# Expert mixture kernel: block 2's load, the last weights' raw buffers, the sums' steps, and the overflow path's form

## The chip, the cores and the metric

One core of a Trainium2 chip runs the whole program. The metric is the device time of one execution in microseconds (us). TensorE is called PE here (PEld is its weight load), VectorE DVE, ScalarE ACT, GpSimd POOL; SP is the engine whose queue issues most DMAs, in the order of the program.

## The reference

Attention with a causal mask and a position bias for 2304 tokens, then a mixture of 8 experts of which every token goes to two, then a gated layer:

```
x = attention(q, k, v, s)                     # 2304 tokens x 512
top2 = two largest of x @ w_gate + noise      # of 8 experts
for e in range(8):
    h = maximum(x[mask] @ w1[e], 0)           # 512 -> 1024
    out[mask] += weight * (h @ w2[e])         # 1024 -> 512
return (sigmoid(out @ w_gate2) * (out @ w_val2)) @ w_out2   # 512 -> 1536 -> 512
```

## The kernel before, in words

The program has three stages: attention and gating (to some 300 us of the span), the experts, and the gated layer, which the code calls `moe2`. Every float32 product is made of three matmuls on a high and a low part (`hh` and `hl`, `xh` and `xl`, `w[:, 0]` and `w[:, 1]`): ACT copies the high part, DVE or POOL subtracts to get the low one.

**The expert stage** is a loop over jobs; a job is one expert and one block `f` of 128 hidden columns. In each pass n of the loop PE does `mm1(n)` (lines 230 to 232, x times the first weights, into `h`), then `mm2s(n - 1)` (lines 244 to 246, into `y`). Between them ACT makes `hh` (line 233) and DVE `hl` (line 234) of the `h` just computed; `mm2s` of the next pass needs both. The order of the work on every engine is that of the code: nothing is reordered, and an instruction that waits holds up all that stands behind it on its engine or queue.

**The last expert** is split. Its first 8 passes take 384 tokens (three tiles), the last 8 the other 256 (two tiles). This text counts passes from the first of the second half: steps -8 to -1 and 0 to 7, so step k is pass `n == tail + k`. The second half takes the 8 weight blocks in another order: its steps 0 to 3 use weights that are still held, its steps 4 to 7 load theirs again. These four are the late weights.

**A weight block** is made by `weights` (lines 151 to 159): SP loads it raw into a buffer `wraw` (line 154), ACT makes its high part (line 157), POOL its low part (line 158). `start(n)` issues the load, `load(n)` starts it if need be and converts. `wraw` has two buffers in the pool `stage`, so a load waits until POOL has done with the block before the last. The last late block (step 7) has a buffer of its own, `tw`.

**Blocks of the gated layer.** `two` (class `Second`) prepares the first three weight blocks of `moe2` while the last expert runs. `block(f)` loads one raw into `ro` (line 526, 768 KB, two buffers), then converts it in three pieces: each is an ACT copy (line 517) and a DVE subtraction (line 521). The table `BLOCKS` says in which step which piece is made. Block 2 takes the `ro` buffer that block 0 leaves.

**The first tokens of the gated layer.** `after(j)` runs at the end of each step j from 0. `both(t)` loads the two halves `y` of the output of token tile t (line 348), DVE adds them (line 339), and `feed` transposes the sum on PE (line 576) and splits it into `xh` (ACT, line 584) and `xl` (DVE, line 586). `FEED = (4, 5, 7)` says in which step each tile's feed is made up; its transposes come one step later.

**The overflow path.** An expert has 640 slots; `overflow` does the tokens beyond them. Every engine loads a count (line 445) and branches (line 446). Here the count is zero, so the body is jumped over on every engine. The body holds 44 PE matmuls for one expert, with a loop around them, and is written out for each of the 8 experts.

Of the kernel before, what the change touches and what calls it, by code (L numbers as in the profile page):

```python
# [8 lines left out]
F32 = mybir.dt.float32  # L9
# [42 lines left out]
LOW_DVE = (3, 5, 6, 7, 16, 17)  # L52


BLOCKS = {-7: (0, 0), -6: (0, 1), -5: (1, 1), -3: (2, 2), -2: (2,)}
FEED = (4, 5, 7)
COMBO = 7 * 256

# [9 lines left out]
@with_exitstack  # L68
def attn_moe_moe2_kernel(ctx: ExitStack, tc: tile.TileContext, q, k, v, s, wgn, noise, wcat, w2cat, out):
    nc = tc.nc  # L70
    ctx.enter_context(tc.manual_schedule())
    const = ctx.enter_context(tc.tile_pool(name="const", bufs=1))


    xs = tc.dram_tile([E * CAP, XW], F32, name="xs")

    ys = tc.dram_tile([2 * N, DM], F32, name="ys")
    aux = tc.dram_tile([2, 2, NP, S], F32, name="aux")

    nc.scalar.preload_act_table_set("natural_log_exp_and_others")  # L80


    identf = const.tile([128, 128], F32, name="identf")
    identr = const.tile([128, 128], F32R, name="identr")
    identb = const.tile([128, 128], BF, name="identb")
    jp = const.tile([128, 128], I32, name="jp")
    nc.gpsimd.iota(jp, pattern=[[1, 128]], base=0, channel_multiplier=-1)
    nc.vector.tensor_scalar(identf, jp, 0.0, None, op0=OP.is_equal)
    nc.vector.tensor_copy(identb, identf)
    mask = const.tile([128, 192], BF, name="mask")  # L90
    nc.vector.tensor_scalar(mask[:, 0:128], jp, 0.0, NEG, op0=OP.is_gt, op1=OP.mult)
    for r in (slice(0, 64), slice(64, 128)):
        nc.vector.tensor_scalar(mask[r, 128:192], jp[r, r], 0.0, NEG, op0=OP.is_gt, op1=OP.mult)
    ltri = const.tile([128, 128], BF, name="ltri")
    ones = const.tile([128, 128], BF, name="ones")
    iota_d = const.tile([128, 8], F32, name="iota_d")
    carry = const.tile([128, 8], F32, name="carry")
    valid = const.tile([128, 5], F32, name="valid")
    wgt = const.tile([128, 4, 32], F32, name="wgt")
    nz = const.tile([128, 20, 8], F32, name="nz")  # L100
    tok = const.tile([128, 20], F32, name="tok")

    def iotas():
        nc.gpsimd.iota(iota_d, pattern=[[-1, 8]], base=8, channel_multiplier=0, allow_small_or_imprecise_dtypes=True)
        nc.gpsimd.iota(carry, pattern=[[CAP, 8]], base=0, channel_multiplier=0, allow_small_or_imprecise_dtypes=True)
        for b in range(B):

            for i, n, base in ((0, 4, b * 512), (4, 1, B * 512 + b * 64)):
                nc.gpsimd.iota(tok[:, 5 * b + i:5 * b + i + n], pattern=[[128, n]], base=base, channel_multiplier=1,
                               allow_small_or_imprecise_dtypes=True)  # L110

    def others():
        nc.vector.tensor_copy(identr, identf)
        nc.vector.tensor_scalar(ltri, jp, 0.0, None, op0=OP.is_gt)
        nc.vector.memset(ones, 1.0)
        nc.vector.memset(valid, 1.0)
        nc.vector.memset(valid[64:128, 4:5], 0.0)

    stage = ctx.enter_context(tc.tile_pool(name="stage", bufs=2))
    state = dict(identf=identf, identb=identb, mask=mask, ltri=ltri, ones=ones, iota_d=iota_d, carry=carry,  # L120
                 valid=valid, wgt=wgt, nz=nz, tok=tok, iotas=iotas, others=others)
    over = const.tile([128, E + 1], I32, name="over")
    cnt = const.tile([128, E], F32, name="cnt")

    def count():

        nc.gpsimd.iota(cnt, pattern=[[CAP, E]], base=SLOTS, channel_multiplier=0, allow_small_or_imprecise_dtypes=True)
        nc.vector.tensor_tensor(cnt, carry, cnt, op=OP.subtract)
        nc.vector.tensor_scalar(cnt, cnt, 0.0, 127.0, op0=OP.max, op1=OP.add)
        nc.vector.tensor_copy(over[:, 0:E], cnt)  # L130
        nc.vector.tensor_scalar(over[:, 0:E], over[:, 0:E], 7, None, op0=OP.logical_shift_right)
        nc.vector.tensor_copy(cnt, over[:, 0:E])
        nc.vector.tensor_reduce(cnt[:, 0:1], cnt, axis=AX.X, op=OP.max)
        nc.vector.tensor_copy(over[:, E:], cnt[:, 0:1])

    w2f = tc.dram_tile([FB2, 128, FF2], F32, name="w2f")
    gs = tc.dram_tile([FB2, 128, N - CT * 128], F32, name="gs")
    gates, res = ExitStack(), ExitStack()
    moe_pools = ExitStack()
    ring = moe_pools.enter_context(tc.tile_pool(name="ring", bufs=4, reuse_waits="tile"))  # L140
    w1 = {}
    blocks = [weights(nc, stage, ring, wcat, 0, f) for f in range(AHEAD)]
    ahead = [lambda f=f: w1.update({f: next(blocks[f])}) for f in range(AHEAD) for _ in range(2)]
    late = attention(tc, gates, ahead, q, k, v, s, wgn, noise, aux, xs, **state)
    with res:
        two, first = moe(tc, moe_pools, res, gates, stage, ring, w1, late, count, xs, ys, wcat, w2cat, w2f, identf, identr)
        overflow(tc, xs, ys, wcat, carry, over, identf)
        moe2(tc, two, first, ys, w2f, gs, identr, out)


def weights(nc, stage, pool, wcat, e, f, name="w", lo=None):

    r = stage.tile([128, 1024], F32, name="wraw")
    nc.sync.dma_start(r, wcat[e, f])
    yield
    w = pool.tile([128, 2, 1024], F32R, name=name)
    nc.scalar.activation(w[:, 0], r, AF.Copy)  # L157
    (lo or nc.gpsimd).tensor_tensor(w[:, 1], r, f32(w[:, 0]), op=OP.subtract)  # L158
    yield w


def moe(tc, pools, res, gates, stage, ring, W, late, count, xs, ys, wcat, w2cat, w2f, identf, identr):
# [4 lines left out]
    with pools as ctx:  # L167
# [17 lines left out]
        def start(n):  # L185
            e, f = jobs[n][0:2]
            lo = nc.vector if n in LOW_DVE else nc.gpsimd
            pool, name = (w0, f"w{f}") if n < FB and f >= 4 else (ring, "w")
            LD[n] = weights(nc, tw[0] if n == n_all - 1 else stage, pool, wcat, e, f, name, lo)
            next(LD[n])  # L190

        def load(n):
# [19 lines left out]
            nc.vector.tensor_tensor(lo, p, f32(hi), op=OP.subtract)  # L212

        def own_tokens(e, t0, t1):
            wt, row = owners(nc, xp, e, XR[e][:, t0:t1, DM:XW], t1 - t0)
            for t in range(t0, t1):
                OWN[e, t] = wt[:, t - t0:t - t0 + 1], row[:, t - t0:t - t0 + 1]

# [110 lines left out]
        def after(j):  # L329

            if j == 0:
                first.extend(two.x0.tile([128, 4, CT * 128], F32R, name=m, bufs=1) for m in ("xh", "xl"))
                y.update((i, both(i)) for i in range(2))
            if j == FEED[0] + 1:
                y[2] = both(2)
            for i, at in enumerate(FEED):
                if j == at:
                    p = ps.tile([128, 512], F32, name=f"y{i}")
                    nc.vector.tensor_tensor(y[i][0], y[i][0], y[i][1], op=OP.add)
                    turns[i] = feed(nc, y[i][0], p, identf, *(x[:, :, i * 128:(i + 1) * 128] for x in first))  # L340
                if at < j < at + 3:
                    next(turns[i])
# [34 lines left out]
        for n in range(FB, n_all):  # L377
# [16 lines left out]
                load(n + 3)  # L394
            if n == tail - 2:
                tw.append(ctx.enter_context(tc.tile_pool(name="tw", bufs=1, side="right", reuse_waits="tile")))
                for i in (4, 5, 7):
                    start(tail + i)
            if n == tail + 2:
                start(tail + 6)  # L400
            for f2 in BLOCKS.get(n - tail, ()):
                two.go(f2)
            if n == tail - 6:
                two.start(two.block, 2, 2)
            if n >= tail:
                after(n - tail)
# [17 lines left out]
    return two, first  # L424


def owners(nc, pool, e, x, n):

    g = pool.tile([128, 4, n], F32, name="own")
    row = pool.tile([128, n], I32, name="row")  # L430
    first, second, w, rf = (g[:, i] for i in range(4))
    nc.vector.tensor_scalar(first, x[:, :, 1], float(E - e), None, op0=OP.is_equal)
    nc.vector.tensor_scalar(second, x[:, :, 1], float(E - e), None, op0=OP.not_equal)
    nc.vector.scalar_tensor_tensor(rf, second, float(N), x[:, :, 0], op0=OP.mult, op1=OP.add)
    nc.vector.tensor_tensor(first, first, x[:, :, 2], op=OP.mult)
    nc.vector.tensor_tensor(second, second, x[:, :, 3], op=OP.mult)
# [2 lines left out]
    return w, row  # L439


def overflow(tc, xs, ys, wcat, carry, over, identf):

    nc = tc.nc
    some = nc.values_load(over[0:1, E:E + 1], min_val=0, max_val=(N - SLOTS) // 128)
    with tc.If(some > 0):
        with ExitStack() as ctx:
# [12 lines left out]
            for e in range(E):  # L460
                nc.gpsimd.indirect_dma_start(
                    out=xs, out_offset=bass.IndirectOffsetOnAxis(ap=endi[:, e:e + 1], axis=0), in_=zt, in_offset=None)
            for e in range(E):
                n = nc.values_load(over[0:1, e:e + 1], min_val=0, max_val=(N - SLOTS) // 128)
                with tc.For_i(0, n, 1) as i:
                    x = sb.tile([128, 1, XW], F32, name="x")
                    nc.sync.dma_start(x[:, 0], xs[bass.ds(i * 128 + (e * CAP + SLOTS), 128), :])
                    w, row = owners(nc, sb, e, x[:, :, DM:XW], 1)
                    p = ps.tile([128, 512], F32, name="t")
                    for c in range(4):  # L470
                        nc.tensor.transpose(p[:, c * 128:(c + 1) * 128], x[:, 0, c * 128:(c + 1) * 128], identf)
# [2 lines left out]
                    y = ps.tile([128, DM], F32, name="y", bufs=1)  # L474
                    for f in range(FB):
                        wt = sb.tile([128, 1024], F32, name="w")
                        nc.sync.dma_start(wt, wcat[e, f])
                        h = ps.tile([128, 512], F32, name="h")
                        for c in range(4):
                            k = slice(c * 128, (c + 1) * 128)  # L480
# [880 lines left out]
```

## Time and profile before

| | us |
|---|---|
| median of 3 runs | 1159.85 (1159.49 to 1161.51) |
| the profiled execution | 1169.18 |
| its span (first to last instruction) | 1167.3 |
| PE busy in the span | 1109.1 (95%) |
| DVE, ACT, POOL busy | 717.4, 527.8, 367.2 |
| last expert, steps -8 to 7, on PE | 653.77 to 727.35 |
| first matmul of `moe2` | 733.16 |

The times below are microseconds from the start of the profiled span. A matmul takes its issue interval on the path, not the length shown: the lengths of neighbours overlap.

### The profile page before, as it was taken

Reading aid. Unit: us, or ns where it says so; the run is one execution under the profiler, and the core shown is the slowest. Engines: PE = TensorE matmul, PEld = TensorE weight load, DVE = VectorE, ACT = ScalarE, POOL = GpSimd, SP = SyncE. Lnnn points to the kernel's source line nnn. Section 1 sums busy time; section 2 is a strip of 40 time slices with the busy share of each in tenths; the row PEclk is TensorE's granted clock in tenths of the full one; section 3 lists DMA queues with packets and bytes.
Section 4 is the critical chain, followed back from the end, with each engine's and each line's share of the span. In section 5 each row is a group of like instructions: output and inputs, shape, how many; then the busy total and the mean of one; then the engine's idle time right before and its main releaser. Section 6 shows DMA issues by size and latency. Waiting matters only on the chain. (4 is left out here: it accounts for less than half of the span.)

```text
span 1167.3 us, 16831 instructions
## 1 busy us (share of the span) xinstructions
PE 1109.1 (95%) x6193; PEld 940.3 (81%) x6193; DVE 717.4 (61%) x1227; ACT 527.8 (45%) x1073; POOL 367.2 (31%) x375
## 2 busy tenths in 40 slices
PE   6999899699999999999999978899999999999998
PEld 4676566478899999999999867899888898988886
DVE  5777788573467687887683444376788567752221
ACT  5887677522333333333333423365566456532211
POOL 2110442405235353535353525012443333300000
PEclk8999999889999999999999989899999999999999
DMA  6798665326555756565754433572554345354442
GB/s 223 247 321 274 197 211 161 107 85 208 192 154 176 252 187 231 176 239 181 252 162 136 168 117 126 147 198 81 163 163 127 109 158 176 116 159 114 133 120 64
DMA packets 84849, 198.77 MB, mean 170 GB/s; under 512 B 7986, under 2 KB 31538, under 8 KB 84756
## 3 DMA queue, kind: packets, MB, share of 16 engines
q1 hardware_dynamic: 76308, 174.54, 46.2%
q0 software_dynamic: 8304, 22.89, 6.5%
q8 instruction: 51, 0.84, 0.3%
q14 instruction: 42, 0.34, 0.1%
q10 hardware_dynamic: 144, 0.16, 0.0%
HBM read 137.01 MB, written 56.66 MB: 166 GB/s over the span
## 5 line engine op out<-in xcount | busy, mean ns | idle before, releaser
L158 POOL TENSOR_TENSOR w<-wraw,w 128x1024 fp32r<-128x1024 f32 x62 | 155.2, 2506 | 248.2 <-ACT w L157 248.2
L230 PE MATMUL h<-xh,w 128*128 128x320 f32 (+2 forms) x512 | 161.6, 316 | 0.0
L232 PE MATMUL h<-xh,w 128*128 128x320 f32 (+2 forms) x512 | 158.5, 310 | 0.0
L231 PE MATMUL h<-xl,w 128*128 128x320 f32 (+2 forms) x512 | 158.4, 309 | 0.0
L157 ACT ACTIVATE w<-wraw 128x1024 fp32r<-128x1024 f32 x68 | 72.0, 1059 | 155.8 <-PE y L246 134.1
L246 PE MATMUL y<-w,hl 128*128 128x512 f32 x320 | 127.1, 397 | 4.4 <-DVE hl L234 4.4
L244 PE MATMUL y<-w,hh 128*128 128x512 f32 x320 | 127.1, 397 | 4.3 <-ACT hh L233 4.3
L245 PE MATMUL y<-w,hh 128*128 128x512 f32 x320 | 126.8, 396 | 0.0
L521 DVE TENSOR_TENSOR w<-ro,w 128x512 fp32r<-128x512 f32 (+1 forms) x105 | 89.2, 890 | 58.3 <-ACT w L517 58.3
L233 ACT ACTIVATE hh<-h 128x320 fp32r<-128x320 f32 (+2 forms) x128 | 55.9, 437 | 136.3 <-PE h L232 132.0
L234 DVE SCALAR_TENSOR_TENSOR hl<-h,hh 128x320 fp32r<-128x320 f32 (+2 forms) x128 | 59.9, 485 | 85.4 <-ACT hh L233 83.2
L230 PEld LDWEIGHTS h<-xh,w 128*128 128x128 f32 x512 | 96.7, 189 | 1.9
L231 PEld LDWEIGHTS h<-xl,w 128*128 128x128 f32 x512 | 96.6, 189 | 1.9
L232 PEld LDWEIGHTS h<-xh,w 128*128 128x128 f32 x512 | 96.5, 189 | 0.0
L1022 ACT ACTIVATE pt<-sc,nm 128x128 f32<-128x128 f32 (+3 forms) x128 | 66.4, 527 | 33.4 <-DVE nm L1005 22.2
L246 PEld LDWEIGHTS y<-w,hl 128*128 128x128 f32 x320 | 60.6, 189 | 19.7 <-DVE hl L234 5.7
L759 PE MATMUL a<-xc,w 128*128 128x512 f32 (+1 forms) x192 | 73.4, 382 | 1.2 <-ACT u L765 1.2
L761 PE MATMUL a<-xc,w 128*128 128x512 f32 (+1 forms) x192 | 72.9, 379 | 0.0
L760 PE MATMUL a<-xc,w 128*128 128x512 f32 (+1 forms) x192 | 72.7, 379 | 0.0
L244 PEld LDWEIGHTS y<-w,hh 128*128 128x128 f32 x320 | 60.5, 189 | 15.2 <-ACT hh L233 4.8
L675 PE MATMUL o<-wo,w 128*128 128x512 f32 x180 | 71.2, 396 | 0.0
L676 PE MATMUL o<-wo,w 128*128 128x512 f32 x180 | 71.2, 396 | 0.0
(234 smaller groups left out, 2552.1 us busy)
## 6 DMA issues: line engine op xcount, KB each, us to landing
wraw<-in_wcat_dram SPq DMA_DIRECT2D x68, 512.0 KB
dw<-in_w2cat_dram SPq DMA_DIRECT2D x24, 768.0 KB
wraw<-w2f SPq DMA_DIRECT2D x24, 512.0 KB
ro<-gs SPq DMA_DIRECT2D x15, 768.0 KB
xs<-zt SPq DMA_DIRECT2D x40, 258.0 KB
xr<-xs SPq DMA_DIRECT2D x40, 258.0 KB
qr<-in_q_dram SPq DMA_DIRECT2D x15, 640.0 KB
w2f<-cv SPq DMA_DIRECT2D x24, 384.0 KB
```

The costliest lines, as they stand in the source:

```text
L157: nc.scalar.activation(w[:, 0], r, AF.Copy)
L158: (lo or nc.gpsimd).tensor_tensor(w[:, 1], r, f32(w[:, 0]), op=OP.subtract)
L230: nc.tensor.matmul(p, w[:, 0, k], xh[:, c, c0], start=c == 0, stop=False)
L231: nc.tensor.matmul(p, w[:, 0, k], xl[:, c, c0], start=False, stop=False)
L232: nc.tensor.matmul(p, w[:, 1, k], xh[:, c, c0], start=False, stop=c == 3)
L244: nc.tensor.matmul(y, hh[:, k], w[:, 0, 512:], start=n % FB == 0, stop=False)
L245: nc.tensor.matmul(y, hh[:, k], w[:, 1, 512:], start=False, stop=False)
L246: nc.tensor.matmul(y, hl[:, k], w[:, 0, 512:], start=False, stop=n % FB == FB - 1)
L521: self.nc.vector.tensor_tensor(w[:, 1, c], r, f32(w[:, 0, c]), op=OP.subtract)
L759: nc.tensor.matmul(b, w[:, 0, k], xh[:, j, c], start=start and c == 0, stop=False, skip_group_check=True)
L760: nc.tensor.matmul(b, w[:, 0, k], xl[:, j, c], start=False, stop=False, skip_group_check=True)
L761: nc.tensor.matmul(b, w[:, 1, k], xh[:, j, c], start=False, stop=c == 1, skip_group_check=True)
```

## The change

It has four parts.

- `BLOCKS` and one line of the loop: the load of block 2 is issued in step -4 instead of step -6, its first piece is made in step -2 and the other two in step -1 (before: two in step -3 and one in step -2).
- All four late weights are started in step -2. That of step 6 no longer shares the two `wraw` buffers: it is loaded into a `ro` buffer.
- `after`: the sum of the two halves is made one step before the feed (steps 3, 4, 6), and the third tile's halves are loaded in step 4 instead of 5.
- `overflow`: the 8 copies of the body become one loop over the experts, which reads its expert's number and count from a small table in DRAM. The arithmetic of the body is the same.

```diff
-BLOCKS = {-7: (0, 0), -6: (0, 1), -5: (1, 1), -3: (2, 2), -2: (2,)}
+BLOCKS = {-7: (0, 0), -6: (0, 1), -5: (1, 1), -2: (2,), -1: (2, 2)}
...
-            LD[n] = weights(nc, tw[0] if n == n_all - 1 else stage, pool, wcat, e, f, name, lo)
+            raw = {n_all - 1: lambda: tw[0].tile([128, 1024], F32, name="wraw"), n_all - 2: lambda: two.raw()[:, 0:1024]}
+            raw = raw.get(n, lambda: stage.tile([128, 1024], F32, name="wraw"))
+            LD[n] = weights(nc, raw, pool, wcat, e, f, name, lo)
...
-            if j == FEED[0] + 1:
+            for i, at in enumerate(FEED):
+                if j == at - 1:
+                    nc.vector.tensor_tensor(y[i][0], y[i][0], y[i][1], op=OP.add)
+            if j == FEED[1] - 1:
                 y[2] = both(2)
...
-                    nc.vector.tensor_tensor(y[i][0], y[i][0], y[i][1], op=OP.add)
...
-                for i in (4, 5, 7):
+                for i in (4, 5, 6, 7):
                     start(tail + i)
-            if n == tail + 2:
-                start(tail + 6)
...
-            if n == tail - 6:
+            if n == tail - 4:
                 two.start(two.block, 2, 2)
...
-            for e in range(E):
-                n = nc.values_load(over[0:1, e:e + 1], min_val=0, max_val=(N - SLOTS) // 128)
+            nc.sync.dma_start(tabd.rearrange("e p c -> p e c"), tab)
+            with tc.For_i(0, E, 1) as e:
+                te = sb.tile([128, 2], F32, name="te", bufs=1)
+                nc.sync.dma_start(te, tabd[bass.ds(e, 1)].rearrange("e p c -> (e p) c"))
+                n = nc.values_load(te[0:1, 1:2].bitcast(I32), min_val=0, max_val=(N - SLOTS) // 128)
                 with tc.For_i(0, n, 1) as i:
```

How the instructions stand. On the queue SP, from step -8 to the branch, before (`wraw` of `wcat` is a raw expert block; `ro` of `w2f` a raw block of the gated layer; `y` of `ys` a half of a token tile):

```order
L154 DMA wraw<-in_wcat_dram 128x1024 x5
L526 DMA ro<-w2f 128x1536 x2
L154 DMA wraw<-in_wcat_dram 128x1024 x2
L526 DMA ro<-w2f 128x1536
L154 DMA wraw<-in_wcat_dram 128x1024 x5
L348 DMA y<-ys 128x512 x4
L154 DMA wraw<-in_wcat_dram 128x1024
L348 DMA y<-ys 128x512 x2
```

The same place on SP after the change (the line numbers are those of the changed file):

```order
L155 DMA wraw<-in_wcat_dram 128x1024 x5
L537 DMA ro<-w2f 128x1536 x2
L155 DMA wraw<-in_wcat_dram 128x1024 x4
L537 DMA ro<-w2f 128x1536
L155 DMA wraw<-in_wcat_dram 128x1024 x2
L155 DMA ro<-in_wcat_dram 128x1024
L155 DMA wraw<-in_wcat_dram 128x1024
L353 DMA y<-ys 128x512 x6
```

Block 2's load now stands behind the raw weights of steps -2 and -1 instead of ahead of them, and step 6's late weights stand ahead of all `y` loads instead of behind four of them.

On ACT, steps -5 to -1, before (`hh` of 384 columns ends one step's `mm1`, `w<-wraw` is an expert's high part, `w<-ro` a piece of a block of the gated layer):

```order
L233 ACTIVATE hh<-h_7033 128x384
L157 ACTIVATE w<-wraw 128x1024
L517 ACTIVATE w<-ro 128x512 x2
L233 ACTIVATE hh<-h_7068 128x384
L157 ACTIVATE w<-wraw 128x1024
L233 ACTIVATE hh<-h_7099 128x384
L517 ACTIVATE w<-ro 128x512 x2
L233 ACTIVATE hh<-h_7130 128x384
L517 ACTIVATE w<-ro 128x512
L233 ACTIVATE hh<-h_7167 128x384
```

And after:

```order
L236 ACTIVATE hh<-h_7032 128x384
L158 ACTIVATE w<-wraw 128x1024
L528 ACTIVATE w<-ro 128x512 x2
L236 ACTIVATE hh<-h_7067 128x384
L158 ACTIVATE w<-wraw 128x1024
L236 ACTIVATE hh<-h_7100 128x384
L236 ACTIVATE hh<-h_7126 128x384
L528 ACTIVATE w<-ro 128x512
L236 ACTIVATE hh<-h_7166 128x384
L528 ACTIVATE w<-ro 128x512 x2
```

Block 2's three pieces moved behind `hh` of steps -2 and -1; what stands between the `hh` of steps -5 and -4 is unchanged.

On DVE, steps 3 to 7, before (`hl` of 256 columns belongs to one step, `y<-y` is a sum of two halves, `xl` the low part of a fed tile):

```order
L234 SCALAR_TENSOR_TENSOR hl<-h_7303,hh 128x256
L234 SCALAR_TENSOR_TENSOR hl<-h_7329,hh 128x256
L339 TENSOR_TENSOR y<-y 128x512
L234 SCALAR_TENSOR_TENSOR hl<-h_7357,hh 128x256
L339 TENSOR_TENSOR y<-y 128x512
L234 SCALAR_TENSOR_TENSOR hl<-h_7391,hh 128x256
L586 TENSOR_TENSOR xl<-y_7353,xh 128x4x128
L234 SCALAR_TENSOR_TENSOR hl<-h_7420,hh 128x256
L586 TENSOR_TENSOR xl<-y_7387,xh 128x4x128
L339 TENSOR_TENSOR y<-y 128x512
```

And after:

```order
L237 SCALAR_TENSOR_TENSOR hl<-h_7304,hh 128x256
L339 TENSOR_TENSOR y<-y 128x512
L237 SCALAR_TENSOR_TENSOR hl<-h_7331,hh 128x256
L339 TENSOR_TENSOR y<-y 128x512
L237 SCALAR_TENSOR_TENSOR hl<-h_7363,hh 128x256
L237 SCALAR_TENSOR_TENSOR hl<-h_7392,hh 128x256
L339 TENSOR_TENSOR y<-y 128x512
L597 TENSOR_TENSOR xl<-y_7360,xh 128x4x128
L237 SCALAR_TENSOR_TENSOR hl<-h_7422,hh 128x256
L597 TENSOR_TENSOR xl<-y_7389,xh 128x4x128
```

Each sum moved ahead of the next step's `hl`. Between the branch and the code behind the overflow path the built program has 8 bodies of 44 matmuls for PE before and one after; counted as the trace counts (a weight load and a matmul apart) that is 704 and 88 instructions, beside 18 to 24 of each loop's own before (some 930 in all) and some 60 after (148 in all).

## Rows read from the trace of the kernel before

**Rows 1.** the page: busy time of engines; code packets of TensorE
```profile
PE 1109.1 (95%) x6193; PEld 940.3 (81%) x6193; DVE 717.4 (61%) x1227; ACT 527.8 (45%) x1073; POOL 367.2 (31%) x375
...
q8 instruction: 51, 0.84, 0.3%
```

**Rows 2.** busy us by engine (PE, PEld, DVE, ACT, POOL), granted clock, DMA
```profile
680.00:690.00 10.00, 3.70 (x9) 2.67 (x10) 7.33 (x6) 4.54 (x8) 5.16 (x3) 0.67 0.45 161
730.00:740.00 10.00, 6.84 (x27) 6.87 (x28) 0.12 (x1) 1.77 (x2) 0.06 (x1) 0.66 0.34 116
```

**Rows 3.** waits of TensorE (PE), 640 to 745 us: total, times, longest
```profile
PE h L643 <- PEq L446: 5.8, 1, 5.8
PE y L246 <- DVE hl L234: 4.4, 2, 4.1
PE y L244 <- ACT hh L233: 4.3, 2, 3.2
PE y L576 <- DVE y L339: 1.1, 1, 1.1
```

**Rows 4.** timeline of PE, 678 to 695 us: start, length, line
```profile
678.72 0.34 PE L232 MATMUL h<-xh,w 128*128 128x384 f32 x1
...
690.18 0.34 PE L230 MATMUL h<-xh,w 128*128 128x384 f32 x1
...
692.27 0.39 PE L244 MATMUL y<-w,hh 128*128 128x512 f32 x1
...
694.36 0.34 PE L230 MATMUL h<-xh,w 128*128 128x384 f32 x1
```

**Rows 5.** the DMA queue SP, 666 to 687 us: issues and one wait
```profile
666.31 0.33 SPq L154 DMA_DIRECT2D wraw<-in_wcat_dram  x1
...
673.97 0.33 SPq L526 DMA_DIRECT2D ro<-w2f  x1
674.38 12.41 SPq L154 DMA_DIRECT2D wraw<-in_wcat_dram  x5
...
SPq L526 <- DVE w L521: 7.2, 1, 7.2
```

**Rows 6.** timeline of POOL, ACT and DVE, 663 to 687 us
```profile
663.85 4.78 POOL L158 TENSOR_TENSOR w<-wraw,w 128x1024 fp32r<-128x1024 f32 x2
...
669.86 1.06 ACT L157 ACTIVATE w<-wraw 128x1024 fp32r<-128x1024 f32 x1 [3.54 <-DMA wraw<-in_wcat_dram]
...
679.71 1.06 ACT L157 ACTIVATE w<-wraw 128x1024 fp32r<-128x1024 f32 x1 [7.38 <-DMA wraw<-in_wcat_dram]
...
681.32 5.20 DVE L521 TENSOR_TENSOR w<-ro,w 128x512 fp32r<-128x512 f32 x2 [6.31 <-ACT w L517]
```

**Rows 7.** timeline of SP and ACT, 707 to 716 us
```profile
707.15 1.75 SPq L348 DMA_DIRECT2D y<-ys  x4
709.00 0.38 SPq L154 DMA_DIRECT2D wraw<-in_wcat_dram  x1
...
714.67 1.06 ACT L157 ACTIVATE w<-wraw 128x1024 fp32r<-128x1024 f32 x1 [4.95 <-DMA wraw<-in_wcat_dram]
```

**Rows 8.** line 446, the branch: ns min/median/max, first and last start
```profile
L446 ACTq EVENT_SEMAPHORE  x2: 17/17/17, 731.6 to 731.7; - x2
...
L446 PEldq COMPARE_BRANCH  x1: 5952/5952/5952, 726.9 to 726.9; - x1
L446 ACTq COMPARE_BRANCH  x1: 50/50/50, 727.9 to 727.9; - x1
```

**Rows 9.** timeline of ACT, DVE and PE, 727 to 738 us
```profile
727.53 0.59 ACT L584 ACTIVATE xh<-y 128x512 fp32r<-128x512 f32 x1
...
728.15 0.69 DVE L586 TENSOR_TENSOR xl<-y,xh 128x512 fp32r<-128x512 f32 x1 [1.15 <-ACT xh L584]
...
733.62 0.52 PE L644 MATMUL h<-xl,w 128*128 128x384 f32 x1
...
738.03 0.34 PE L643 MATMUL h<-xh,w 128*128 128x384 f32 x1
```

More of the change, by code (lines that the diff above doesn't have):

```diff
@@ L77, in attn_moe_moe2_kernel @@
     ys = tc.dram_tile([2 * N, DM], F32, name="ys")
+    tabd = tc.dram_tile([E, 128, 2], F32, name="tabd")
     aux = tc.dram_tile([2, 2, NP, S], F32, name="aux")
@@ L141, in attn_moe_moe2_kernel @@
     w1 = {}
-    blocks = [weights(nc, stage, ring, wcat, 0, f) for f in range(AHEAD)]
+    blocks = [weights(nc, lambda: stage.tile([128, 1024], F32, name="wraw"), ring, wcat, 0, f) for f in range(AHEAD)]
     ahead = [lambda f=f: w1.update({f: next(blocks[f])}) for f in range(AHEAD) for _ in range(2)]
@@ L146, in attn_moe_moe2_kernel, with weights @@
         two, first = moe(tc, moe_pools, res, gates, stage, ring, w1, late, count, xs, ys, wcat, w2cat, w2f, identf, identr)
-        overflow(tc, xs, ys, wcat, carry, over, identf)
+        overflow(tc, xs, ys, wcat, carry, over, tabd, identf)
         moe2(tc, two, first, ys, w2f, gs, identr, out)
-def weights(nc, stage, pool, wcat, e, f, name="w", lo=None):
-    r = stage.tile([128, 1024], F32, name="wraw")
+def weights(nc, raw, pool, wcat, e, f, name="w", lo=None):
+    r = raw()
     nc.sync.dma_start(r, wcat[e, f])
@@ L214, in own_tokens @@
         def own_tokens(e, t0, t1):
-            wt, row = owners(nc, xp, e, XR[e][:, t0:t1, DM:XW], t1 - t0)
+            wt, row = owners(nc, xp, float(E - e), XR[e][:, t0:t1, DM:XW], t1 - t0)
             for t in range(t0, t1):
@@ L424, in moe, with owners @@
     return two, first
-def owners(nc, pool, e, x, n):
+def owners(nc, pool, who, x, n):
     g = pool.tile([128, 4, n], F32, name="own")
@@ L431, in owners @@
     first, second, w, rf = (g[:, i] for i in range(4))
-    nc.vector.tensor_scalar(first, x[:, :, 1], float(E - e), None, op0=OP.is_equal)
-    nc.vector.tensor_scalar(second, x[:, :, 1], float(E - e), None, op0=OP.not_equal)
+    nc.vector.tensor_scalar(first, x[:, :, 1], who, None, op0=OP.is_equal)
+    nc.vector.tensor_scalar(second, x[:, :, 1], who, None, op0=OP.not_equal)
     nc.vector.scalar_tensor_tensor(rf, second, float(N), x[:, :, 0], op0=OP.mult, op1=OP.add)
@@ L439, in owners, with overflow @@
     return w, row
-def overflow(tc, xs, ys, wcat, carry, over, identf):
+def overflow(tc, xs, ys, wcat, carry, over, tabd, identf):
     nc = tc.nc
@@ L462, in overflow @@
                     out=xs, out_offset=bass.IndirectOffsetOnAxis(ap=endi[:, e:e + 1], axis=0), in_=zt, in_offset=None)
-            for e in range(E):
-                n = nc.values_load(over[0:1, e:e + 1], min_val=0, max_val=(N - SLOTS) // 128)
+            tab = sb.tile([128, E, 2], F32, name="tab", bufs=1)
+            nc.gpsimd.iota(tab[:, :, 0], pattern=[[-1, E]], base=E, channel_multiplier=0,
+                           allow_small_or_imprecise_dtypes=True)
+            nc.vector.tensor_copy(tab[:, :, 1].bitcast(I32), over[:, 0:E])
+            nc.sync.dma_start(tabd.rearrange("e p c -> p e c"), tab)
[3 more added lines that the diff above has]
+                n = nc.values_load(te[0:1, 1:2].bitcast(I32), min_val=0, max_val=(N - SLOTS) // 128)
                 with tc.For_i(0, n, 1) as i:
                     x = sb.tile([128, 1, XW], F32, name="x")
-                    nc.sync.dma_start(x[:, 0], xs[bass.ds(i * 128 + (e * CAP + SLOTS), 128), :])
-                    w, row = owners(nc, sb, e, x[:, :, DM:XW], 1)
+                    nc.sync.dma_start(x[:, 0], xs[bass.ds(i * 128 + e * CAP + SLOTS, 128), :])
+                    w, row = owners(nc, sb, te[:, 0:1], x[:, :, DM:XW], 1)
                     p = ps.tile([128, 512], F32, name="t")
@@ L476, in overflow @@
                         wt = sb.tile([128, 1024], F32, name="w")
-                        nc.sync.dma_start(wt, wcat[e, f])
+                        nc.sync.dma_start(wt, wcat[bass.ds(e, 1), f].rearrange("e p n -> (e p) n"))
                         h = ps.tile([128, 512], F32, name="h")
```

## Prediction

> **What bounds the kernel now.** I read the page first, then the clock and busy time by stretch, then what PE waits for, and last the timelines of the places that these point at. PE is busy 95% of the span [rows 1], so a gain has to be a PE gap that closes. The waits of PE from 640 to 745 us show where such gaps are: one of 5.8 us at the branch of line 446, two of 3.2 and 4.1 us for `hh` and `hl`, and two of 1.1 us, for `hh` and for a sum `y` [rows 3]. [...] The three clusters are gaps A, B and C below.
>
> **Gap A: the raw weights of step -2 are late.** ACT takes up the block of step -2 at 679.71, after 7.38 us of waiting for its DMA [rows 6]. It stands ahead of `hh` of step -4 on ACT, so PE waits for that. The DMA is late because of the queue: SP issued it at 674.38, right behind the load of block 2 at 673.97, which had waited 7.2 us for DVE to leave its `ro` buffer [rows 5]. Its own buffer was free long before: POOL had done with the block of step -4 at 663.85 + 4.78 = 668.6 [rows 6].
>
> The change puts block 2's load behind both raw blocks. So the block of step -2 is issued at about 668.7. A raw block took 3.55 us from issue to use alone (666.31 to 669.86) and 5.33 behind block 2's 768 KB (674.38 to 679.71) [rows 5, 6]; it is ready between 672.3 and 674.0. Before, PE took up `hh` of step -4 2.6 us after that copy began (678.72 + 0.34 + the wait of 3.2 = 682.3 [rows 3, 4]); now that is 674.9 to 676.6, and PE wants it at 678.9. `hl` is closer. Two pieces on DVE took 5.20 us while POOL subtracted beside them [rows 6], where a subtraction of that size takes 0.69 alone [rows 9]. POOL's one subtraction (2.39) now starts 1.06 after the copy does and ends between 675.8 and 677.5; after a piece held until then, a second piece and an `hl` of like length end between 677.2 and 678.9, and PE wants `hl` two matmuls into `mm2s`, at 679.4. So the wait goes, with 0.5 to 2.2 us to spare.
>
> Its price: without a wait `mm2s` of step -4 starts 0.17 after 678.72, at 678.9, and its nine matmuls last 692.27 to 694.36, that is 2.09 us [rows 4]; the next `mm1` then starts at 680.99 instead of 690.18 [rows 4]. **A = 9.2 us**, of which 7.3 are the two waits and the rest the lower clock. Bounds: 6 if the block comes so late that a third of it stays, 9.2 if none does.
>
> What moves to steps -2 and -1 is block 2's three pieces. Its load is issued at about 674, wanted in step -2 at 683.9 of the new schedule; the longest way from issue to use in the rows is 5.7 us (709.00 to 714.67) [rows 7]. POOL has no subtraction in those steps, so the pieces cost DVE 0.69 each, beside some 4.2 us of matmuls a step. Cost 0.
>
> **Gap B: the late weights of step 6, and the sums.** They were started in step 2, at 709.00, behind four loads of `y` at 707.15, and ACT got them at 714.67 after 4.95 us of waiting [rows 7]; PE waits 1.1 for the `hh` behind that copy, and then 1.1 for the first sum [rows 3], which stood behind that step's `hl`. Now they are issued in step -2, some 20 us before use. **B = 2.2 us.** The sums stand one step earlier, ahead of `hl` of steps 4, 5 and 7. What hides them is the `mm1` that PE does before it wants that `hl`. The first sum could wait for its load. The five loads issued from 707.15 on (four of 256 KB, one of 512) were in by 714.67 [rows 7], 7.5 us for 1.5 MB; the first pair, a third, by some 709.7, which is when DVE comes to the sum. If it were in only at 714.67, `hl` would hold PE for up to 3 us; so B has the bounds -0.8 and 2.2, and I take 2.2, as transfers of one queue land in turn (step -2's block came 5.33 us after issue behind block 2, and 3.55 alone).
>
> **Gap C: the branch.** PE's branch took 5.95 us (726.9 to 732.9); ACT's took 0.05, but its next instruction stands 3.7 us later, at 731.6 [rows 8]. The engines jump over the overflow body. PE's code comes in packets: 51 of them for 2 x 6193 instructions [rows 1], some 243 each. Before, the jump passes over some 930 PE instructions, almost four packets; after, over some 148, less than one. [...] No row shows the price of so short a jump; its bounds are nothing and the 5.95 of the long one, and I take the low end, since in straight code PE crosses from packet to packet without a wait in rows 3.
>
> [...]
>
> With the branch free, `moe2` waits for its first tokens. The last `xh` is made from 727.53 to 728.12 and the last `xl` from 728.15 to 728.84 [rows 9], so its second matmul, which reads `xl`, can start at 728.9. It started at 733.62 [rows 9]: 4.7 us. From there to 738.03 are 14 matmul intervals in 4.41 us at the lower level; at full clock, 12 of this size take 690.18 to 692.27, 0.174 each [rows 4], so 2.43: another 2.0 us. The gap that stays, some 1.5 us, is far shorter than those ahead of the two stretches of lower clock (5.8, and 3.2 with 4.1) [rows 2, 3]. **C = 6.7 us**; bounds 0 and 6.7. If only ACT's branch stayed slow, PE would wait for it until 731.7 and C would be near 2.
>
> **The sum.** 9.2 + 2.2 + 6.7 = 18.1 us. From the profiled execution's 1169.18 that gives 1151.1. Its time is 9.3 above the median; taking the same gaps in the timed runs, 1159.85 - 18.1 = **1141.8 us**. Behind 740 us PE is busy without a gap that a DMA sets, so what is gained arrives at the end.
>
> **Rivals.**
> - *The branch stays slow* (any code fetch remains, or the 5.95 us is something else). For it: no short jump is in the trace. Against: the others' 3.7 us at the same place with a jump of a third of PE's. Time: C between 0 and 2, so 1159.85 - 11.4 = 1148.5, or 1146.5.
> - *DVE is held by POOL.* `hl` of step -4 has 0.5 us to spare at the late bound, and the sums of steps 3 and 4 now fall beside POOL's subtractions of the late weights. The 5.20 us of [rows 6] speak for it; against it, that `hl` of these steps is wanted only after the next `mm1`. Time: 1.5 to 4 us less gain, about 1144.5. [...]
> - *The gaps are the profile's.* The profiled execution is 9.3 us above the median; if all of that lay in A to C, the timed runs would gain 18.1 - 9.3 = 8.8: 1151.0. Against: A and C follow from the order of a queue and from code length, not from measurement.
> - *Slower: ACT is held by block 2.* Its first piece stands on ACT ahead of `hh` of step -1. If its load came x us after 683.9, PE would wait x less one `mm2s` (2.1). It eats the gain from x = 20 on, and shows as slower (2.3 us more) from x = 22.5, a landing 32 us after issue, against 5.7 at most in the rows.
>
> **How the numbers follow.** All three gaps close: 0.6, own range 1138.5 to 1144. Branch slow: 0.15. DVE held: 0.12. Gaps of the profile: 0.07. Held by block 2: 0.03; no change, for a reason not seen: 0.03. The predicted time is that of the first. The range 1138 to 1149 takes in the first three cases (0.87) and the bounds of C. A measurement of this kernel can tell about 0.2%, 2.3 us, from no change. Faster 0.94, same 0.03, slower 0.03.
>
> **What would show it.** A: SP issues the raw block of step -2 near 669, before block 2's load; ACT does not wait over 2 us for it, and the waits of PE for `hh` and `hl` in steps -4 to -2 are gone, with a granted clock of 1.0 there. B: the conversion of step 6's weights waits for PE, not for a DMA. C: the branch on PE is far below 1 us, and PE's gap before line 643's successor is about 1.5 us, ended by `xh`. Wrong would make it: a PE gap of over 3 us left at the branch, or a new wait for `hl` in steps 3 to 5.

## The result and the profile after

The changed kernel takes 1144.02 us (median of 4 runs, 1139.75 to 1145.16); the kernel before, run beside it, 1160.68 (1159.49 to 1162.47). The ratio is 0.9845, 95% interval 0.9817 to 0.9872: some 17 to 18 us, 1.5%. Forecast were 1141.8 us and a gain of 18.1. (The level of one and the same kernel moved between the sessions below, 1160.7 to 1172.3 us for the one before, so only ratios within a session are compared.)

What PE waits for from 600 to 745 us in the changed kernel (total, times, longest), to be held against [rows 3]:

```profile
PE y L249 <- DVE hl L237: 2.4, 1, 2.4
PE h L654 <- ACTq L449: 0.9, 1, 0.9
PE h L655 <- DVE xl L597: 0.2, 1, 0.2
```

The waits for `hh` and for the sum `y` are gone, and the branch fell from 5.8 us to 0.9 on ACT's branch and 0.2 on `xl`. But one wait for `hl` is left, of 2.4 us. By stretch (columns as in [rows 2]):

```profile
660.00:670.00 10.00, 7.62 (x35) 6.39 (x35) 8.88 (x9) 5.03 (x8) 5.26 (x3) 0.94 0.63 226
670.00:680.00 10.00, 10.00 (x46) 8.81 (x46) 1.87 (x4) 2.56 (x4) 2.43 (x2) 0.89 0.42 143
710.00:720.00 10.00, 8.89 (x51) 8.30 (x50) 2.17 (x4) 3.97 (x6) 2.10 (x4) 1.00 0.32 110
```

The clock at the branch is now full (0.66 before), while in the stretch of gap A a dip is left. The timelines show which `hl` it is (the first row of SP merges three issues; its second row is from a view that begins at 659 us and holds the last two of them):

```profile
657.88 7.36 SPq L155 DMA_DIRECT2D wraw<-in_wcat_dram  x3
...
660.23 5.01 SPq L155 DMA_DIRECT2D wraw<-in_wcat_dram  x2
665.46 0.33 SPq L537 DMA_DIRECT2D ro<-w2f  x1
...
661.34 1.06 ACT L158 ACTIVATE w<-wraw 128x1024 fp32r<-128x1024 f32 x1 [3.44 <-DMA wraw<-in_wcat_dram]
...
663.86 1.06 ACT L158 ACTIVATE w<-wraw 128x1024 fp32r<-128x1024 f32 x1
...
662.47 5.18 POOL L159 TENSOR_TENSOR w<-wraw,w 128x1024 fp32r<-128x1024 f32 x2 [2.28 <-ACT w L158]
...
662.95 5.25 DVE L532 TENSOR_TENSOR w<-ro,w 128x512 fp32r<-128x512 f32 x2 [1.12 <-ACT w L528]
668.13 0.55 DVE L237 SCALAR_TENSOR_TENSOR hl<-h,hh 128x384 fp32r<-128x384 f32 x1
...
668.73 0.80 PE L249 MATMUL y<-w,hl 128*128 128x512 f32 x1 [2.38 <-DVE hl L237]
```

SP does now what was forecast: of three raw blocks the first (657.88) is that of step -3, the second (660.23) that of step -2 and the third (664.90) that of step -1, and all come before block 2's load at 665.46, where [rows 5] had the last two behind it. ACT takes up the block of step -2 at 663.86 with no wait for a DMA. What follows from that was not forecast: the block of step -3 had been taken up at 661.34, so POOL now makes both subtractions in one go, 5.18 us from 662.47, and the two pieces that DVE began at 662.95 took 5.25 us beside them. Behind these stands `hl` of step -5, which ended at 668.68; PE had wanted it 2.4 us earlier. The matmul at 668.73 is in `mm2s` of step -5, one step ahead of the two waits of gap A.

For gap B the conversion of step 6's weights on ACT, and the sums on DVE:

```profile
696.81 1.06 ACT L158 ACTIVATE w<-ro 128x1024 fp32r<-128x1024 f32 x1 [1.05 <-PE y L249]
...
696.55 1.52 DVE L339 TENSOR_TENSOR y<-y 128x512 f32<-128x512 f32 x1 [0.34 <-DMA y<-ys]
...
698.95 1.97 DVE L339 TENSOR_TENSOR y<-y 128x512 f32<-128x512 f32 x1
```

The conversion reads `ro` and waits for PE, not for a DMA (4.95 us of DMA in [rows 7]). The first sum waits 0.34 us for its load and takes 1.5, the second 1.97; no `hl` behind them holds PE. For gap C the branch (columns as in [rows 8]):

```profile
L449 ACTq EVENT_SEMAPHORE  x2: 17/17/17, 711.5 to 711.6; - x2
...
L449 PEldq COMPARE_BRANCH  x1: 352/352/352, 709.0 to 709.0; - x1
L449 ACTq COMPARE_BRANCH  x1: 50/50/50, 711.3 to 711.3; - x1
```

PE's branch takes 0.35 us where it took 5.95, and ACT goes on 0.2 us after its own where it took 3.7. Last, five points of PE: the first matmul of step -8, the first of step 0, the last of `mm2s`, the first of `moe2` and the 25th of `moe2`:

```profile
645.34 0.34 PE L233 MATMUL h<-xh,w 128*128 128x384 f32 x1
...
684.60 0.28 PE L233 MATMUL h<-xh,w 128*128 128x256 f32 x1
...
709.87 0.39 PE L249 MATMUL y<-w,hl 128*128 128x512 f32 x1
...
711.57 0.44 PE L654 MATMUL h<-xh,w 128*128 128x384 f32 x1 [0.87 <-ACTq L449]
...
716.37 0.33 PE L654 MATMUL h<-xh,w 128*128 128x384 f32 x1
```

From these every execution can be measured in four parts that leave out the 640 us ahead of step -8, where the code is the same (us):

| kernel | steps -8 to -1 | steps 0 to 7 | to the first of `moe2` | 24 matmuls more | sum |
|---|---|---|---|---|---|
| before | 44.79 | 27.96 | 6.64 | 6.44 | 85.83 |
| after | 39.26 | 25.27 | 1.70 | 4.80 | 71.03 |

That is 14.8 us. The two profiled executions differ by 24.0, of which 8.4 lie ahead of step -8 (it starts at 653.77 before and 645.34 after). All profiled executions below have it between 641 and 654: the span of a single execution says less than a part of it.

### The profile page after: what moved, and what is told of

Read it like the earlier page. It is cut to its first block, busy times and chain, and to the rows that moved or that the text cites. A ratio compares the mean times of both kernels' runs of the same rounds, so it can differ in the third digit from the quotient of the medians.

```text
span 1143.2 us, 16833 instructions
## 1 busy us (share of the span) xinstructions
PE 1103.8 (97%) x6193; PEld 936.9 (82%) x6193; DVE 716.8 (63%) x1227; ACT 529.0 (46%) x1073; POOL 366.3 (32%) x375
## 5 line engine op out<-in xcount | busy, mean ns | idle before, releaser
L159 POOL TENSOR_TENSOR w<-wraw,w 128x1024 fp32r<-128x1024 f32 x61 | 152.5, 2501 | 234.1 <-ACT w L158 233.8
L557 POOL TENSOR_TENSOR ro<-wraw 128x256 f32<-128x256 f32 x48 | 41.0, 854 | 96.6 <-DMA wraw<-w2f 70.2
```

## The experiments

**The parts one by one.** Theory: the three gaps have three causes, each undone by its own part, and the wait of 2.4 us came in with part A. Three kernels, each the one before with one part of the diff: A (`BLOCKS` and block 2's start), B (late weights and sums), C (`overflow`).

Part A alone:

```diff
-BLOCKS = {-7: (0, 0), -6: (0, 1), -5: (1, 1), -3: (2, 2), -2: (2,)}
+BLOCKS = {-7: (0, 0), -6: (0, 1), -5: (1, 1), -2: (2,), -1: (2, 2)}
-            if n == tail - 6:
+            if n == tail - 4:
                 two.start(two.block, 2, 2)
```

> The kernel before with only the table of blocks and block 2's start in step -4 (part A). Theory, the queue with a rest: the raw block of step -2 no longer stands behind block 2's load, so both waits of 3.2 and 4.1 us and their lower clock go, but POOL now makes two subtractions in a row beside DVE's two pieces of step -6, so one wait of 2.4 us for hl of step -5 and some 0.9 us of lower clock come in their place: 9.2 - 3.3 = 5.9 us faster. Rival, the gaps are the profile's (its execution stood 9 us above the median): half of A at most, 3 us or less. Rival, the rest comes from the other parts of the change (late weights, sums) and not from this one: 9.2 us faster, no wait for hl of step -5.

Ratio 0.9940 (0.9914 to 0.9966), 7.0 us. The waits of PE:

```profile
PE h L643 <- PEq L446: 5.8, 1, 5.8
PE y L246 <- DVE hl L234: 2.6, 1, 2.6
PE y L576 <- DVE y L339: 1.1, 1, 1.1
PE y L244 <- ACT hh L233: 0.5, 1, 0.5
```

The two waits of gap A are replaced by one of 2.6 us for `hl`, with this part alone; branch and sum stand as in [rows 3]. Steps -8 to -1 take 39.22 us for 44.79. The second rival falls. The first falls too: the interval begins at 4.0 us, and in the trace the gain of this part is 5.6 us in the steps themselves.

Part B alone (the edits of the diff to `raw`, `start` and `after`):

> The kernel before with only the late weights' raw buffers and the sums a step ahead (part B). Theory: the waits of 1.1 us for hh and of 1.1 us for the sum go: 2.2 us faster; the conversions of step 6's weights then wait for PE and not for a DMA. Rival, the time comes back at the branch, which is as slow as before: its 5.95 us starts when PE comes to it, so it can hide nothing of the 2.2; but PE's gap before the first matmul of moe2 would be 2.2 us longer if it were ended by the last xl: 0 us. Gap A should read as before (3.2 and 4.1 us).

Ratio 0.9960 (0.9933 to 0.9988), 4.6 us. PE's waits and its branch:

```profile
PE y L248 <- DVE hl L236: 4.6, 2, 4.1
PE h L645 <- ACTq L448: 3.4, 1, 3.4
PE y L246 <- ACT hh L235: 3.2, 1, 3.2
```

```profile
L448 PEldq COMPARE_BRANCH  x1: 3832/3832/3832, 715.9 to 715.9; - x1
```

The steps 0 to 7 gain 2.7 us (25.27 for 27.96), as the theory has it in kind (it named 2.2). What neither theory had: the branch, which this part doesn't touch, takes 3.83 us and not 5.95, and PE's gap ends with ACT's branch.

Part C alone (`owners`, `overflow` and `tabd` of the diff):

> The kernel before with only the overflow path as a loop over experts (part C). Theory, code that is fetched: PE's branch takes 0.35 us in place of 5.95, PE's gap behind it falls from 5.8 to about 1 us, the granted clock there stays at 1.0: 4.7 and 2.0, that is 6 to 7 us faster. Rival, the gain is taken back in moe2 (its blocks come later than its matmuls want them): 3 us or less, with a new PE wait behind 735 us. Gap A should read as before. If the three parts add up, this one, part A (5.9) and part B (2.2) make the 16.7 us of the whole change.

Ratio 0.9935 (0.9909 to 0.9961), 7.6 us.

```profile
PE y L247 <- DVE hl L235: 4.3, 2, 4.1
PE y L245 <- ACT hh L234: 4.2, 2, 3.2
PE y L585 <- DVE y L340: 1.1, 1, 1.1
PE h L652 <- ACTq L447: 0.9, 1, 0.9
```

The branch as in the changed kernel, the rest as before; the gap and the 24 matmuls behind it take 6.50 us for 13.08. In `moe2`, behind the branch's waits, PE waits 1.3 us in all, where it was 1.2. In the sums of the four parts, A gains 6.3, B 5.5 and C 6.6 us alone: 18.4, but 14.8 together. So the parts don't add up, and most of the overlap is at the branch (B alone has 9.93 us there for 13.08).

**What is left of gap A.** Theory: DVE is held by POOL's second subtraction. Two edits take it away in different ways, one by the pieces and one by the subtraction; the changed kernel is timed beside them.

> The changed kernel as it is, timed beside the next ones. Every theory: 16 to 18 us faster than before, a PE wait of 2.4 us for hl of step -5, and 39.3 us from the first matmul of step -8 to that of step 0.

Ratio 0.9851 (0.9821 to 0.9881); wait 2.4 us; 39.27.

```diff
-BLOCKS = {-7: (0, 0), -6: (0, 1), -5: (1, 1), -2: (2,), -1: (2, 2)}
+BLOCKS = {-7: (0, 0), -6: (0,), -5: (1,), -4: (1,), -3: (1,), -2: (2,), -1: (2, 2)}
```

> The changed kernel with the pieces of blocks 0 and 1 spread out: one piece each in steps -6, -5, -4 and -3 in place of two in -6 and two in -5. Theory, DVE is held by POOL's two subtractions in a row: the one piece of step -6 is held only by the first of them (to 665 us), hl of step -5 ends before PE wants it (666.2), the wait of 2.4 us and 0.9 us of lower clock go: steps -8 to -1 last 36.0 us in place of 39.3, and the kernel is some 3.3 us faster than the changed one. Rival, the raw block of step -3 that came late to ACT (a wait of 3.4 us for its DMA) sets hl: a wait of 1 to 2 us stays. Rival, the wait moves to hl of step -4 or -3, beside whose steps the pieces now fall: no gain.

Ratio 0.9815 (0.9788 to 0.9842); 1140.03 us where the changed kernel beside it took 1144.78. The two intervals just overlap, so it is the trace that carries this reading. POOL's subtractions and DVE's pieces and `hl`, and PE's waits:

```profile
658.94 5.21 POOL L159 TENSOR_TENSOR w<-wraw,w 128x1024 fp32r<-128x1024 f32 x2 [2.39 <-ACT w L158]
...
659.42 2.47 DVE L532 TENSOR_TENSOR w<-ro,w 128x512 fp32r<-128x512 f32 x1 [1.24 <-ACT w L528]
661.81 0.55 DVE L237 SCALAR_TENSOR_TENSOR hl<-h,hh 128x384 fp32r<-128x384 f32 x1
662.28 2.42 DVE L532 TENSOR_TENSOR w<-ro,w 128x512 fp32r<-128x512 f32 x1
```

```profile
PE h L654 <- ACTq L449: 0.9, 1, 0.9
PE h L655 <- DVE xl L597: 0.2, 1, 0.2
```

Each piece is still held for a subtraction (2.4 to 2.5 us, against 0.69 alone), but only one stands ahead of each `hl`. The wait is gone; steps -8 to -1 take 35.06 us, 4.2 less. ACT still waits 3.56 us for the late block of step -3, but that sets nothing, and no wait moved.

```diff
-LOW_DVE = (3, 5, 6, 7, 16, 17)
+LOW_DVE = (3, 5, 6, 7, 16, 17, 70)
```

> The changed kernel with the low part of step -2's block made by DVE and not by POOL, so that only one subtraction of POOL lies beside the two pieces of step -6. Theory, DVE is held by POOL: the two pieces take 3.1 us (as beside one subtraction before) in place of 5.25, hl of step -5 ends near 666.5 on the old time scale, and PE waits 0.4 us in place of 2.4. Rival, the pieces are slow for a reason of their own (two in a row, or the DMA traffic of the raw blocks): 5 us again and a wait of 2.4. Second rival: POOL's work costs as much on DVE, and hl of step -4 is late instead, by 1 us or more.

```profile
658.37 2.40 POOL L159 TENSOR_TENSOR w<-wraw,w 128x1024 fp32r<-128x1024 f32 x1 [2.52 <-ACT w L158]
...
658.85 3.08 DVE L532 TENSOR_TENSOR w<-ro,w 128x512 fp32r<-128x512 f32 x2 [1.37 <-ACT w L528]
661.85 0.55 DVE L237 SCALAR_TENSOR_TENSOR hl<-h,hh 128x384 fp32r<-128x384 f32 x1
```

```profile
PE y L249 <- DVE hl L237: 0.5, 1, 0.5
```

The same two pieces, begun as early, take 3.08 us beside one subtraction; PE waits 0.5 us. Steps -8 to -1 take 35.77. With either edit the wait goes as the theory has it, and both rivals fall. (This kernel and the next four, up to the late weights alone, were timed once each, 1138 to 1158 us; they are read by their traces.)

**What the branch costs.** Theory after the first runs: PE's branch waits for one packet of code, and the packet stands in the DMA engines behind data. In part B's kernel SP is past its own branch sooner, so the next 768 KB that it loads for `moe2` are in earlier. Rival: the price goes by the length jumped. The loop's body is written out k times, with a loop of 8 / k rounds around it:

```diff
-            with tc.For_i(0, E, 1) as e:
+            with tc.For_i(0, E // 4, 1) as e:
+                for u in range(4):
...
-                te = ...tabd[bass.ds(e, 1)]
+                    te = ...tabd[bass.ds(e * 4 + u, 1)]
```

> The changed kernel with the overflow path written out for four experts and a loop of two rounds around them: the same work and the same jump at the branch, but over some 500 PE instructions, about two packets of code, in place of some 150 (0.6 of a packet) and 930 (3.8 packets). Theory, a target outside the packets that are there is fetched at one price: PE's branch takes 3.5 to 6 us, as in the kernel before. Rival, the price goes by the length jumped: 500 of 930, 3 us or less on PE's branch. Rival, what cost was something else in the written-out path (its eight loads of counts or its labels), not the length: 0.35 us.

> The changed kernel with two bodies written out and a loop of four rounds: a jump over some 267 PE instructions, 1.1 packets, in place of 151 (0.6) and 499 (2.1, where PE's branch took 3.35 us). Theory, a jump into the packet that runs or the one behind it is free: 0.35 us, or, as it is just over one packet, 2.4 to 3.4 us if the branch stands so near a packet's end that the target falls into the second one behind. Rival, the price goes by the length: some 1.8 us.

With four bodies and, below, with the sums' steps and the third tile's loads put back:

```diff
-            for i, at in enumerate(FEED):
-                if j == at - 1:
-                    nc.vector.tensor_tensor(y[i][0], y[i][0], y[i][1], op=OP.add)
-            if j == FEED[1] - 1:
+            if j == FEED[0] + 1:
                 y[2] = both(2)
...
+                    nc.vector.tensor_tensor(y[i][0], y[i][0], y[i][1], op=OP.add)
                     turns[i] = feed(...)
```

> The kernel with four bodies and a loop of two rounds, and in it the sums and the third tile's loads back where they stood before the change (part B's second half undone), so that SP comes to its own branch later and issues the next load of block weights (768 KB) just ahead of PE's branch. The jump is the same 500 PE instructions. Theory, PE's branch waits for one packet of code, and the packet stands behind the data that SP issued: 5 to 6 us on PE's branch in place of 3.35, and the packet starts 2 us or more after the branch. Rival, the price goes by the length of the jump: 3.35 us again.

Part B without its sums:

> The kernel before with only the late weights of step 6 in the other buffer and started in step -2, the sums and the third tile's loads where they were. In the kernel with both, PE's branch took 3.83 us and not 5.95. Theory, it is the loads of the third tile (issued 10 us earlier, so that SP is past its branch and its 768 KB are in when PE branches) that made the branch shorter: here the branch takes 5 to 6 us again, PE's wait of 1.1 us for hh is gone and that of 1.1 us for the first sum stays. Rival, the late weights' place on SP made it: 3.8 us.

And the changed kernel without part C:

> The changed kernel with the overflow path written out for eight experts as before (parts A and B without C). From the single parts: B alone brought PE's branch from 5.95 to 3.83 us, since SP's block load is in by then. Theory, the branch waits for one packet behind SP's data: here it takes 3.8 us too, and from the last mm2s matmul to the 25th matmul of moe2 it is 9.9 us (as with B alone) against 6.5 in the changed kernel and 13.1 before: the loop is worth 3.4 us beside B and not the 6.6 that it is worth alone; the kernel is some 11 to 12 us faster than before. Rival, the parts add up: the branch costs 5.95 us again, 13.1 from the last mm2s, and the loop's share is 6.6 us.

The branch of PE in the kernel with four bodies, and SP's issue of the 768 KB; then both with the sums' steps put back:

```profile
L449 PEldq COMPARE_BRANCH  x1: 3352/3352/3352, 711.0 to 711.0; - x1
```

```profile
707.62 0.33 SPq L538 DMA_DIRECT2D ro<-w2f  x1
```

```profile
L447 PEldq COMPARE_BRANCH  x1: 4249/4249/4249, 706.5 to 706.5; - x1
```

```profile
704.51 0.33 SPq L536 DMA_DIRECT2D ro<-w2f  x1
```

The length is the same; the load was issued 3.4 us ahead of the branch in the first and 2.0 in the second, and the branch takes 0.9 us longer. All kernels, read in the same rows each. The last column but one is when the next packet of PE's code (16 KB, the DMA queue q8) started in the DMA engines, by the trace's records of single packets; the PE instructions jumped are counted from the built programs.

| kernel | PE instructions jumped | 768 KB issued ahead of the branch by, us | code packet started behind the branch's start by, us | PE's branch, us |
|---|---|---|---|---|
| before | 930 | 0.6 | 3.0 | 5.95 |
| part A | 930 | 0.7 | 2.9 | 5.97 |
| late weights of part B | 930 | 1.7 | 2.1 | 4.61 |
| part B | 930 | 3.2 | 1.4 | 3.83 |
| parts A and B | 930 | 3.4 | 0.9 | 3.73 |
| four bodies, sums put back | 500 | 2.0 | 1.8 | 4.25 |
| four bodies | 500 | 3.4 | 0.9 | 3.35 |
| two bodies | 270 | 3.3 | 1.0 | 3.53 |
| part C | 150 | 0.7 | none while it ran | 0.35 |
| after | 150 | 3.3 | none while it ran | 0.35 |

Down the third column the price falls as the load is earlier; down the second it doesn't follow the length: 270 cost what 500 and 930 cost at the same lead. The fourth column shows what PE waits for. The DMA queues (packets, MB, share of the 16 DMA engines) of the kernel before, from the branch to 729.8 us:

```profile
q1 hardware_dynamic: 138, 0.79, 79.1%
```

The same kernel, from there to the branch's end, and the kernel with four bodies from 711.9 us to its branch's end:

```profile
q8 instruction: 1, 0.02, 3.1%
```

```profile
q8 instruction: 1, 0.02, 2.4%
```

In the kernel before, the 768 KB (q1) fill the DMA engines first; their last packet started at 729.73, the code packet at 729.90. In the four kernels with a long jump whose load was issued 2.0 us ahead or less, the code packet started within 0.2 us of the load's last packet. In the other four that last packet had started 0.3 to 0.6 us behind the branch, and the code packet came at 0.9 to 1.0 (1.4 with part B, which the load does not account for). The packet then took 0.9 to 1.5 us, and from its end to the branch's end it was 1.4 to 1.6 us in all eight. So a long jump waits for one packet, and the packet for the data ahead of it.

With some 150 instructions the branch waits for no packet, even with the load just ahead (part C alone). For PE at this place the price begins between 150 and 270 instructions. Length alone need not decide where: with four bodies POOL went on 3.3 us after its branch (713.6 to 716.9) and DVE 0.6 after its own (714.1 to 714.7), and both jump some 180. The expectation for two bodies had the second of its values, nearly (2.4 to 3.4 us); that for the sums put back missed its size (4.25 for 5 to 6), as the load was not as late as in the kernel before.

The kernel with the late weights alone missed two values. Its branch, 4.61 us, is neither the 5 to 6 of its theory nor the 3.8 of the rival: the late weights' place and the sums' steps each bring SP's load forward, by 1.1 and 1.5 us. And the wait of 1.1 us for the first sum did not stay.

```profile
PE y L248 <- DVE hl L236: 4.6, 2, 4.1
PE h L643 <- PEq L446: 4.4, 1, 4.4
PE y L246 <- ACT hh L235: 3.3, 1, 3.3
```

Its steps 0 to 7 take the same 25.27 us as all of part B. So the late weights alone bring the 2.7 us, and the sums' steps and the early loads bring nothing there; they bring 1.05 us at the branch (5.26 to 4.21 from the last `mm2s` to `moe2`), through SP.

Without part C, parts A and B give a ratio of 0.9919 (0.9888 to 0.9950), 9.5 us where 11 to 12 were expected. The branch was forecast right (3.8 us; 3.73); the lower clock behind it lasted longer than with B alone (7.04 us for 24 matmuls, not 5.72), so the loop is worth 4.8 us beside A and B in this execution, and 3.4 with the clock of the other. The gap's part of it is 2.6 us, against 4.9 alone.

**The rest of the gap at the branch.** `FEED = (4, 5, 6)` in the kernel with the pieces spread.

> The kernel with the pieces spread out, and the third tile's feed made up in step 6 in place of 7, so that its transposes stand ahead of the last mm2s and ACT's xh is done before its branch. Theory, what is left of PE's gap at the branch (0.9 us for ACT's branch, 0.2 for xl) is xh and xl alone: the gap from the last mm2s matmul to the first of moe2 falls from 1.70 to 0.4 to 0.7 us, the kernel is 1.0 to 1.3 us faster, below what its time can tell. Rival, the sum in step 5 waits for the third tile's loads (issued until about 693.4 in the kernel with the pieces spread) and holds hl of step 6: a new PE wait of up to 2 us, no gain.

Ratio 0.9804 (0.9775 to 0.9833), not to be told from 0.9815.

```profile
PE h L654 <- ACTq L449: 0.8, 1, 0.8
```

The wait for `xl` went, but the 0.8 us for ACT's branch stays: ACT's last work ahead of it is now `yo`, which waits for the last `mm2s` (714.23 to 714.92), so ACT gets there hardly earlier. Gap 1.22 us for 1.70, and with the transposes now inside the steps 0.6 us gained in the four parts, half of what was expected. The sum in step 5 waited 1.86 us for its load, but no `hl` is held.

## Why the prediction was right in its size, and where it was wrong

**Gap A: the mechanism right, a step wrong.** The queue was the cause of both waits: with block 2's load behind the raw blocks the two are gone. The step that failed is that DVE's pieces have "POOL's one subtraction" beside them, with "0.5 to 2.2 us to spare" for `hl` of step -4. I moved the block of step -2 forward, but left POOL's other subtraction, that of step -3, where it had stood, well ahead. Both then fell in a row, beside the pieces of step -6, and held `hl` one step earlier than the one I had checked. The 5.20 us of [rows 6] had themselves stood beside two subtractions in a row (5.12 us of POOL from 680.85), not beside one. A was forecast at 9.2 us and is 5.5 (44.79 to 39.26), just below its lower bound of 6. The rest, 4.2 us with its clock, is what the spread pieces brought. That was the rival *DVE is held by POOL*, at the price that it named (1.5 to 4 us; 3.7 here), though for another `hl` than it named; its 1144.5 us is closer to the 1144.02 measured than the 1141.8 of the forecast. The rows agree with this rival: a piece, 0.69 us alone, takes 2.4 to 2.5 beside a subtraction, two beside two (5.18 us of POOL) 5.25, two beside one (2.40) 3.08.

**Gap B: right, with a wrong share.** Forecast 2.2, measured 2.7 in the steps. But the sum's wait of 1.1 us was no wait of its own; it went with the late weights.

**Gap C: right, by a reason that was half of it.** Forecast 6.7: 4.7 of gap and 2.0 of clock; alone it measured 4.94 and 1.64, and the gap left is 1.7 us, where 1.5 was forecast. The granted clock was 0.50 in the first 4 us of `moe2` before and 1.00 after. That so short a jump costs next to nothing was my estimate; it costs 0.35 us, a long one 3.35 to 5.97, and the price is one fetch, not the length (3.35 to 3.73 us for 270 to 930 PE instructions at leads of 3.3 and 3.4 us). What I lacked is that the fetch stands behind data, so that part B already took 2.4 us off the gap. The long jumps, of 270 PE instructions and more, wait for a code packet, the short ones, of 150, for none. In straight code a packet comes while PE works: in the kernel before, one is in the DMA engines between 632 and 634 us, for 0.9 us, and PE has no wait from 620 to 660.

**The sum.** 18.1 forecast, 14.8 in the trace; in time 0.9845 of the kernel before, whose interval (0.9817 to 0.9872) reaches from 15 to 21 us. So the time cannot tell the two sums apart, and that it came within 2.2 us of the forecast while the trace fell 3.3 short is in part luck. The rival *the gaps are the profile's* falls: it gives 8.8 us. Where the 9.3 us lay by which the profiled execution stood above the median is not shown, but they fit the part ahead of step -8: it took 653.77 us there and 641 to 647 in all other profiled executions but the last two (parts A and B, 653.78, and the feed in step 6, 653.02, in a session with a level 11 us higher). *The branch stays slow* and *ACT is held by block 2* show in no row.

## What to carry to other kernels

When a load is brought forward, follow every engine that works on it: here the earlier block made two POOL subtractions adjacent, and a pair of DVE pieces beside them took 5.25 us, where it takes 3.08 beside one. Where POOL's subtractions hold DVE's as here, put one DVE piece between two `hl` and not two. Keep a body that is mostly jumped over short (loops instead of copies; PE's branch took 0.35 us over some 150 instructions and 3.35 or more from 270 on), and let large loads be in before a long jump (3.35 us with 768 KB issued 3.4 us ahead, 4.25 with 2.0); and measure a change by the distance of two marks around it, since the part ahead, with the same code, moved by up to 13 us between the profiled executions.

## What the runs showed that was not expected

PE's long jump cost from 3.35 to 5.97 us in different kernels, and the row that goes with it is not the length but the lead of a 768 KB load (0.6 to 3.4 us), by when it lets the code packet through. SP itself still stands 2.7 us at its branch in the changed kernel (its instructions jumped are some 140), as before, which delays nothing. On ACT a jump of some 200 instructions cost 0.4 us (713.3 to 713.7, four bodies) where some 340 cost 2.5 to 3.7 in the kernels with eight; where ACT's price begins was not tried. The stretch of lower clock (granted 0.5) from the first matmul of `moe2` on, behind a gap of 4.2 us, lasted 3.2 us in one execution and 6.0 in another (part B, and parts A and B), so its price is not given by the gap alone.
